# Rounding fp64 weights: the sign bits move from VectorE to GpSimd, the conversion is cut into four pieces, and the first attention pairs are planned closer

## The chip, the core and the metric

The kernel runs on one core of a Trainium2 chip. Its engines are TensorE (PE, with its weight loads as PEld), VectorE (DVE), ScalarE (ACT), GpSimd (POOL) and SyncE (SP), which here issues nearly all DMA transfers. The metric is the device time of one execution in microseconds (us); lower is better.

## What is computed

Two blocks follow each other. The first is attention with RMS-normalised queries and keys, over 8 batches, 12 heads, 448 positions and a head size of 64. The second is a SwiGLU feed-forward on the 3584 x 768 result, with 1536 hidden columns. The three weight matrices come in as fp64 numbers.

```python
q_n, k_n = rmsnorm(q, g_q), rmsnorm(k, g_k)
scores = (1 / sqrt(64)) * matmul(q_n, k_n.T)
attn = softmax(scores)
x = matmul(attn, v)                      # per head, then (B*S, H*D)
g = x @ w_gate
out = (silu(g) * (x @ w_val)) @ w_out
```

## The kernel before, in words

**Stages.** Two heads of a batch are a pair; there are 48. The first 12 pairs (`EARLY`, the first two batches) are computed alone, before any feed-forward. Then come four blocks of the feed-forward, each for two batches: an up part (gate and value products, line 1299) and a down part (line 1473). The attention of the next 12 pairs is woven into the down part of each block. The products use a scheme with 15 sub-products of 3 x 3 blocks: both the activations and the weights are first combined into 15 "sides". One up product is two matmuls of 128 x 448, with 120 products in a block (4 groups of 15 steps for gate and value).

**An early pair.** Queries and keys are loaded (line 728), squared on ACT (754), summed on DVE (768), turned into inverse roots (678 to 686), scaled on GpSimd (795), transposed on DVE (811) and, for queries, scaled again on ACT (814). PE makes the scores (840), ACT the exponentials (855), PE the weighted sums (916) and the sums of the weights (940). DVE takes reciprocals of these (975), PE spreads them over the rows (980), and DVE multiplies (1002). After six pairs DVE makes the activations' sides (1036 and 1040).

**Conversion of weights.** `convert` handles one of 24 parts of the fp64 weights (16 for the up part, 8 for the down part). A part is 128 x 1152 values, loaded as 64-bit words of which `lo` and `hi` are the two 32-bit halves. ACT makes a scaled copy of `hi` that drops the sign's and the exponent's upper part into place (line 1127) and scales `lo` (1131). Then DVE works on two halves of 576 values. For each it shifts the bits left by 3 (1147), takes the sign bit of `hi` and joins it to the bits (1150), and adds the rounded low part as an integer (1153). GpSimd makes the 15 sides of the weights in 12 instructions (1171 and 1174), and one store sends them to DRAM (1199), from where the blocks load them into `ws` (1260).

The first six conversions keep the shifted bits in SBUF. The other 18 (`by_bank`) put them into a PSUM bank (`st`), so that the instructions 1147, 1150 and 1153 have one operand in PSUM. The first conversions run beside the early pairs, all others beside block 0.

**Reads of the product banks.** Up products go to four PSUM banks, which DVE or ACT reads with one instruction for each product (ACT 1242 copies, DVE 1244 adds, 1246 subtracts, 1248 subtracts from the bank). Products of one chain go on accumulating in a bank, and the next may start only when the reading of the one before has ended. When a hidden value is complete ACT applies the silu (1373) and DVE multiplies (1376); line 1350 joins two partial results.

**What sets the order.** All of this is recorded as pieces, each with an engine, a planned duration, a due time and what it must come after. A planner (`Order.run`) walks through the pieces like a list scheduler and emits them one after the other. So it fixes the order of instructions on each engine at build time; each engine then runs its queue in that order, and an instruction that has to wait holds up all that stand behind it. A piece is emitted whole: nothing comes between its instructions on its engine. Due times (`when`) set priorities: the pairs are due `PAIR` us apart from `LEAD` on, and the due time of block 0 (`FIRST`) follows from these. `starts` and `spans` give the due times of the four groups of conversions; those of the second to fourth group are counted from `FIRST`. A piece marked `port` is kept apart from other pieces with that mark[...].

Of the kernel before, what the change touches and what calls it, by code (L numbers as in the profile page):

```python
# [360 lines left out]
class Order:  # L361
# [24 lines left out]
    def add(  # L386
        self, engine, us, when, emit, after=(), takes=(), uses=(), port=False, kb=0, group=None,
        mode=None, early=None, rank=0.0,
    ):
        piece = dict(  # L390
            engine=engine, us=us, when=when, emit=emit, takes=takes, port=port, kb=kb,
            group=group, mode=mode, early=early, rank=rank,
            after=[a for a in after if a is not None], end=None, n=len(self.pieces),
        )
        for tile_of in (*takes, *uses):
            self.users.setdefault(tile_of, []).append(piece)
        self.pieces.append(piece)
        return piece
# [79 lines left out]
def fast(  # L478
# [41 lines left out]
    nc = tc.nc  # L520
# [3 lines left out]
    P = 128  # L524
# [6 lines left out]
    TB = 512  # L531
# [23 lines left out]
    tiles = {}  # L555
# [10 lines left out]
    def take(name, key, shape):  # L566
        if name in ("e", "ea"):
            at = order.turn[name] % BUFS[name]
            tiles[name, key] = es[:, at] if at < BUFS["e"] else more_es[:, at - BUFS["e"]]
            return tiles[name, key]  # L570
        if name in OFTEN:
            at = OFTEN[name] + order.turn[name] % BUFS[name]
            tiles[name, key] = spare[:, ts(at, S)]
            return tiles[name, key]
        if name == "eh":
            at = order.turn["eh"] % BUFS["eh"]
            tiles[name, key] = more[:, at].rearrange("p (h q) -> p h q", h=2)
            return tiles[name, key]
        if name in WORK:
            at, size = WORK[name]  # L580
            at += order.turn[name] % BUFS[name] * size
            n = 1
            for length in shape[1:]:
                n *= length
            x = work[0 : shape[0], at : at + n]
            letters = "abcd"[: len(shape) - 1]
            x = x.rearrange(
                f"p ({' '.join(letters)}) -> p {' '.join(letters)}",
                **dict(zip(letters, shape[1:])),
            )  # L590
            tiles[name, key] = x
            return x
        pool = psum if name in ("st", "at") else sbuf
        tiles[name, key] = pool.tile(shape, F32, name=name, bufs=BUFS[name])
        return tiles[name, key]
# [37 lines left out]

    LEAD, PAIR = 14.0, 10.0
    FIRST = LEAD + EARLY * PAIR + 6.0
    PRODUCT = 1.504
    UP, DOWN, BOTH = 30 * NG * PRODUCT, 90.7, 170.0
# [449 lines left out]
    VALUES = 9 * P  # L1089
# [11 lines left out]
    def convert(key, src, sums, to, when, place, by_bank):  # L1101
# [3 lines left out]
        def add(*what, **more):  # L1105
            return order.add(*what, **dict(rank=rank, **more))
# [17 lines left out]
        bits = dst.bitcast(U32)  # L1124
        one = add(
            "ACT", 1.28, when,
            lambda: nc.scalar.activation(dst, hi.bitcast(F32), AF.Copy, scale=2.0**-111),
            after=[loaded],
        )
        two = add(  # L1130
            "ACT", 1.28, when, lambda: nc.scalar.activation(lo, lo, AF.Copy, scale=2.0**-29),
            after=[loaded],
        )


        bank = ("st", ("bits", key))

        def round_part(k, takes=False):
            if by_bank:
                if k == 0:  # L1140
                    take(*bank, [P, 2, TB])
                part = ts(k, VALUES // 2)
                to = tiles[bank].rearrange("p b t -> p (b t)")[:, 0 : VALUES // 2].bitcast(U32)
            else:
                part = ts(k, VALUES // 2)
                to = bits[:, part]
            nc.vector.tensor_scalar(
                out=to, in0=bits[:, part], scalar1=3, scalar2=None, op0=ALU.logical_shift_left
            )
            nc.vector.scalar_tensor_tensor(  # L1150
                to, hi[:, part], 0x80000000, to, op0=ALU.bitwise_and, op1=ALU.bitwise_or
            )
            nc.vector.tensor_tensor(out=bits[:, part], in0=to, in1=lo[:, part], op=ALU.add)

        last = one
        for k in range(2):
            last = add(
                "DVE", 2.28 if by_bank else 1.85, when, lambda k=k: round_part(k), after=[last, two],
                takes=[bank] if by_bank and k == 0 else [], uses=[bank] if by_bank and k else [],
                port=not by_bank,  # L1160
            )

        blocks = dst.rearrange("p (b f) -> p b f", f=P)
        b21, b31, b13, b23, b11, b12, b22, b32, b33 = (blocks[:, i] for i in range(9))
# [17 lines left out]
        for us, op in (  # L1182
# [21 lines left out]
    def up_weights(i, *how):  # L1204

        g, which, c = i // 4, i // 2 % 2, i % 2
        w = (moe_w_gate, moe_w_val)[which].rearrange("(c k p) (n f) -> p c k n f", p=P, k=3, n=3)
        weights["up", i] = convert(
            ("up", i), lambda k, n: w[:, c, k, n, ts(g, P)], UP_SUMS, up_sides[g][:, :, which, c],
            *how,  # L1210
        )

    def down_weights(i, *how):

        g, s = divmod(i, 2)
# [357 lines left out]
    for i in range(P // C):  # L1573
        h, half = divmod(i, 2)
# [4 lines left out]
            out=gg, in0=gq2, scalar=8.0 * GAIN**-2, in1=gk2, op0=ALU.mult, op1=ALU.mult  # L1579
# [5 lines left out]
    first = [(up_weights, i) for i in range(4 * NG)] + [(down_weights, i) for i in range(2 * NG)]  # L1585
    turns = [(*XS, *GT[:2], HS, SPARE), (ES, PAIRS, GT[2], SPARE, HS), (ES, PAIRS, HS, SPARE), (ES, HS)]
    starts = [LEAD - 4.0, FIRST - 20.0, FIRST + 60.0, FIRST + 110.0]
    spans = [16.0, 8.0, 9.0, 10.0]
    counts = [6, 10, 6, 2]
    todo = iter(first)  # L1590
    for n in range(4):
# [11 lines left out]
def kernel(  # L1603
# [63 lines left out]
```

## Time and profile before

The kernel takes 1500.53 us (median of three runs, 1499.26 to 1501.53). The profiled execution has a span of 1497.2 us.

| engine | busy us | share of the span | instructions |
|---|---|---|---|
| PE (matmul) | 1434.6 | 96% | 6672 |
| DVE | 916.9 | 61% | 1405 |
| ACT | 689.8 | 46% | 1372 |
| GpSimd | 408.8 | 27% | 468 |

| row | count | mean ns of one |
|---|---|---|
| GpSimd 1171, side of weights, 128x128, in es | 25 | 503 |
| GpSimd 1174, two sides, 128x256, in es | 10 | 822 |
| GpSimd 795, scaling of a pair, 128x448 | 96 | 1040 |
| GpSimd 860, sums, 128x896 | 36 | 2170 |
| DVE 975, reciprocals, 128x224, in the first 350 us | 12 | 1552 |
| PE 1299, up product, one matmul of 128x448 (mm) | 960 | 544 |

The first table shows which engine is full over the whole span; a mean over stages with different limits says little of one of them, so what a stage is worth is read from its own window. The second gives what single instructions last. A time in the columns "idle before" of the profile is charged to the wait that ended last, and idle time of an engine that isn't the bottleneck costs nothing by itself.

### The profile page before, as it was taken

To read this page: it belongs to the slowest core of one execution; us is meant where nothing else is said; L and a number is where in the kernel's file an instruction comes from. 1 tells how busy PE (TensorE), PEld (TensorE's weight loads), DVE (VectorE), ACT (ScalarE), POOL (GpSimd) and SP (SyncE) were. 2 spreads that over 40 slices of the span, in tenths; PEclk is the share of its full clock that TensorE was granted. 3 is DMA by queue.
4 is the path that set the end of the run, shared out by engine and by line. 5 is a ranking of instruction groups with operands and counts; after the bars stand their busy time and mean duration, and the time that the engine had idled before them with its cause. 6 is when DMAs were issued, how large, how long until landed. Compare 5 with 4: busy or idle time off the path is not lost.

```text
span 1497.2 us, 19504 instructions
## 1 busy us (share of the span) xinstructions
PE 1434.6 (96%) x6672; PEld 681.5 (46%) x6672; DVE 916.9 (61%) x1405; ACT 689.8 (46%) x1372; POOL 408.8 (27%) x468
## 2 busy tenths in 40 slices
PE   5898999799999999999999999999999999999998
PEld 2333444343344455554444445554444445555553
DVE  5867877868886743455876753453786854423533
ACT  6764544347777422254777432235677532122100
POOL 2562666544454300002344400002344410000000
PEclk9898999999999999999999999999999999999999
DMA  7675999974444342343453442343344343222235
GB/s 168 152 160 166 315 309 309 288 219 99 98 99 109 80 137 71 114 114 88 100 123 82 87 130 84 104 118 104 82 110 109 83 114 106 71 106 70 84 97 106
DMA packets 415922, 193.31 MB, mean 129 GB/s; under 512 B 324164, under 2 KB 397892, under 8 KB 409668
## 3 DMA queue, kind: packets, MB, share of 16 engines
q1 hardware_dynamic: 402688, 190.35, 47.5%
q10 hardware_dynamic: 12996, 1.61, 0.7%
q8 instruction: 55, 0.90, 0.3%
q14 instruction: 55, 0.45, 0.1%
q0 software_dynamic: 128, 0.00, 0.0%
HBM read 157.29 MB, written 34.60 MB: 128 GB/s over the span
## 4 chain that ended last, share of the span: by engine, by line
PE 73%; DVE 3%; ACT 1%; issue 1%; DMA 0%; SPq 0%; DVEq 0%; ACTq 0%
PE mm L1473 22%; PE mm L1299 19%; PE at L1299 19%; PE st L840 6%; PE at L916 6%; PE st L940 1%; DVE ss L684 0%; DMA out_dram<-spare 0%; ACT es L855 0%; DVE sums L866 0%; DVE ss L768 0%; DVE rd L975 0%; DVE ss L782 0%; DVE hs L1040 0%; ACT spare L990 0%
## 5 line engine op out<-in xcount | busy, mean ns | idle before, releaser
L1299 PE MATMUL mm<-xs,ws 128*128 128x448 f32 x960 | 405.0, 544 | 15.9 <-DVE gt L1248 9.9
L1299 PE MATMUL at<-xs,ws 128*128 128x448 f32 x960 | 400.7, 540 | 0.8 <-DVE v L1246 0.7
L1299 PEld LDWEIGHTS mm<-xs,ws 128*128 128x128 f32 x960 | 182.1, 191 | 199.4 <-issue 169.2
L1299 PEld LDWEIGHTS at<-xs,ws 128*128 128x128 f32 x960 | 182.3, 190 | 182.1 <-issue 174.5
L795 POOL TENSOR_TENSOR work<-work,rr 128x448 f32<-128x448 f32 x96 | 97.8, 1040 | 504.7 <-DVE rr L686 345.6
L1473 PE MATMUL mm<-gt,ws 128*128 128x448 f32 x448 | 175.7, 543 | 0.0
L840 PE MATMUL st<-work 64*64 64x448 f32 (+1 forms) x1536 | 154.8, 510 | 21.9 <-ACT work L814 15.6
L1244 DVE TENSOR_TENSOR gt<-gt,mm 128x448 f32<-128x448 f32 x64 | 39.7, 621 | 210.2 <-PE mm L1299 185.7
L1473 PE MATMUL mm<-hs,ws 128*128 128x448 f32 x384 | 151.0, 544 | 0.0
L855 ACT ACTIVATE es<-st 128x896 f32<-128x896 f32 x129 | 114.5, 915 | 75.5 <-PE at L916 52.2
L1373 ACT ACTIVATE st<-gt 128x448 f32<-128x448 f32 x96 | 52.6, 548 | 204.8 <-DVE gt L1248 104.4
L860 POOL TENSOR_TENSOR sums<-es 128x896 f32<-128x896 f32 x36 | 78.1, 2170 | 193.0 <-PE st L940 84.7
L990 ACT COPY spare<-rd 32x224 f32<-32x224 f32 x288 | 108.2, 376 | 47.3 <-DVE rd L975 42.1
L1473 PEld LDWEIGHTS mm<-gt,ws 128*128 128x128 f32 x448 | 83.5, 190 | 83.4 <-issue 80.5
L916 PE MATMUL at<-es,v 64*64 64x448 f32 x1032 | 115.0, 561 | 4.5 <-DVE xs L998 3.3
L1242 ACT COPY gt<-mm 128x448 f32<-128x448 f32 x80 | 42.6, 532 | 162.5 <-PE mm L1299 162.4
L1473 PEld LDWEIGHTS mm<-hs,ws 128*128 128x128 f32 x384 | 71.3, 190 | 71.4 <-issue 69.6
L840 PEld LDWEIGHTS st<-work 64*64 64x64 f32 x1536 | 52.0, 134 | 98.0 <-issue 35.7
L1242 ACT COPY v<-at 128x448 f32<-128x448 f32 x96 | 51.0, 531 | 76.1 <-PE at L1299 75.9
L860 POOL TENSOR_TENSOR sums<-sums,es 128x896 f32<-128x896 f32 x36 | 75.8, 2107 | 6.7 <-ACT es L855 4.1
L811 DVE STREAM_TRANSPOSE work<-work 128x448 f32<-128x448 f32 x96 | 58.7, 628 | 24.6 <-POOL work L795 15.1
L916 PEld LDWEIGHTS at<-es,v 64*64 64x64 f32 x1032 | 40.9, 138 | 67.7 <-issue 59.2
(141 smaller groups left out, 1581.6 us busy)
## 6 DMA issues: line engine op xcount, KB each, us to landing
ws<-up_sides SPq DMA_DIRECT2D x32, 1024.0 KB, 4.9
ws<-down_sides SPq DMA_DIRECT2D x16, 1024.0 KB, 4.9
ws<-down_sides SPq DMA_DIRECT2D x28, 512.0 KB, 4.0
ws<-up_sides SPq DMA_DIRECT2D x16, 768.0 KB, 4.4
work<-in_q_dram SPq DMA_DIRECT2D x192, 56.0 KB, 2.3
work<-in_k_dram SPq DMA_DIRECT2D x188, 56.0 KB, 2.3
out_dram<-spare SPq DMA_DIRECT2D x168, 56.0 KB, 1.9
v<-in_v_dram SPq DMA_DIRECT2D x96, 96.0 KB, 2.4
```

Source lines behind the costliest of these rows:

```text
L795: nc.gpsimd.tensor_tensor(out=tiles["t", m][:, x], in0=tiles["qk", (m, x)], in1=rr.to_broadcast([P, NC, C]), op=ALU.mult,)
L811: nc.vector.transpose(to, tiles["t", m][:, x].rearrange("p c f -> p (c f)"))
L840: nc.tensor.matmul(st[ds(D * x, D), h, 0:n], tiles["KT", m][rows, ds(P * j + D * of_keys, D)], tiles["QT", m][rows, ds(Q * of_queries, n)] ...
L855: nc.scalar.activation(e, tiles["st", (m, j)][:, :, 0 : S * width(j) // P], AF.Exp)
L860: nc.gpsimd.tensor_tensor(out=to, in0=tiles["e", (m, 0)] if j == 1 else to, in1=e, op=ALU.add)
L916: nc.tensor.matmul(tiles["at", (m, x)][ds(D * h, D), queries], tiles["v", m][rows, j, h], tiles["e", (m, j)][rows, h], start=j == 0, stop= ...
L990: nc.scalar.copy(inv[ds(D * h + C * to, C), ts(x, Q)], tiles["rd", m][ds(D * h + C * x, C)])
L1242: nc.scalar.copy(to, ps)
L1244: nc.vector.tensor_tensor(out=to, in0=old, in1=ps, op=ALU.add)
L1299: nc.tensor.matmul(ps(), w[:, at, which, c], xs[:, SLOT[x], c], start=fresh and c == 0, stop=c == NC2 - 1, skip_group_check=True,)
L1373: nc.scalar.activation(take(*act, [P, 2, TB])[:, 0, 0:S], to, AF.Silu)
L1473: nc.tensor.matmul(banks[s][:, 0:S], w[:, at, s, g], where[x][:, g], start=fresh and g == 0, stop=g == NG - 1, skip_group_check=True,)
```

## The change

For each conversion GpSimd now turns `hi` in place into an integer that holds the sign bit alone: it compares with 0 and multiplies by 2^31, with an unsigned integer as output. That is one instruction over all 1152 values. DVE then needs two instructions for each half instead of three: the shift and the joining of the sign become one (`shift`), and the integer addition stays (`round_part`). Each of these is a piece of its own, so that a conversion is four pieces of DVE work where it was two, and the planner may put other work between them. The first pairs are due 9 us apart instead of 10, and the first six conversions 13 us apart instead of 16.

```diff
--- before.py
+++ after.py
@@ -633,7 +633,7 @@
 
 
 
-    LEAD, PAIR = 14.0, 10.0
+    LEAD, PAIR = 14.0, 9.0
     FIRST = LEAD + EARLY * PAIR + 6.0
     PRODUCT = 1.504
     UP, DOWN, BOTH = 30 * NG * PRODUCT, 90.7, 170.0
@@ -1131,34 +1131,46 @@
             "ACT", 1.28, when, lambda: nc.scalar.activation(lo, lo, AF.Copy, scale=2.0**-29),
             after=[loaded],
         )
+        three = add(
+            "POOL", 1.6, when,
+            lambda: nc.gpsimd.tensor_scalar(
+                out=hi, in0=hi.bitcast(F32), scalar1=0.0, scalar2=2.0**31, op0=ALU.is_lt,
+                op1=ALU.mult,
+            ),
+            after=[one], port=True,
+        )
 
 
         bank = ("st", ("bits", key))
 
-        def round_part(k, takes=False):
-            if by_bank:
-                if k == 0:
-                    take(*bank, [P, 2, TB])
-                part = ts(k, VALUES // 2)
-                to = tiles[bank].rearrange("p b t -> p (b t)")[:, 0 : VALUES // 2].bitcast(U32)
-            else:
-                part = ts(k, VALUES // 2)
-                to = bits[:, part]
-            nc.vector.tensor_scalar(
-                out=to, in0=bits[:, part], scalar1=3, scalar2=None, op0=ALU.logical_shift_left
-            )
+        def half(k):
+            part = ts(k, VALUES // 2)
+            if not by_bank:
+                return part, bits[:, part]
+            bank_of = tiles[bank].rearrange("p b t -> p (b t)")
+            return part, bank_of[:, 0 : VALUES // 2].bitcast(U32)
+
+        def shift(k):
+            if by_bank and k == 0:
+                take(*bank, [P, 2, TB])
+            part, to = half(k)
             nc.vector.scalar_tensor_tensor(
-                to, hi[:, part], 0x80000000, to, op0=ALU.bitwise_and, op1=ALU.bitwise_or
-            )
+                to, bits[:, part], 3, hi[:, part],
+                op0=ALU.logical_shift_left, op1=ALU.bitwise_or,
+            )
+
+        def round_part(k):
+            part, to = half(k)
             nc.vector.tensor_tensor(out=bits[:, part], in0=to, in1=lo[:, part], op=ALU.add)
 
         last = one
         for k in range(2):
-            last = add(
-                "DVE", 2.28 if by_bank else 1.85, when, lambda k=k: round_part(k), after=[last, two],
-                takes=[bank] if by_bank and k == 0 else [], uses=[bank] if by_bank and k else [],
-                port=not by_bank,
-            )
+            for x, op in enumerate((shift, round_part)):
+                last = add(
+                    "DVE", 0.77 if by_bank else 0.9, when, lambda k=k, op=op: op(k),
+                    after=[last, two, three], takes=[bank] if by_bank and not k and not x else [],
+                    uses=[bank] if by_bank and (k or x) else [], port=not by_bank,
+                )
 
         blocks = dst.rearrange("p (b f) -> p b f", f=P)
         b21, b31, b13, b23, b11, b12, b22, b32, b33 = (blocks[:, i] for i in range(9))
@@ -1585,7 +1597,7 @@
     first = [(up_weights, i) for i in range(4 * NG)] + [(down_weights, i) for i in range(2 * NG)]
     turns = [(*XS, *GT[:2], HS, SPARE), (ES, PAIRS, GT[2], SPARE, HS), (ES, PAIRS, HS, SPARE), (ES, HS)]
     starts = [LEAD - 4.0, FIRST - 20.0, FIRST + 60.0, FIRST + 110.0]
-    spans = [16.0, 8.0, 9.0, 10.0]
+    spans = [13.0, 8.0, 9.0, 10.0]
     counts = [6, 10, 6, 2]
     todo = iter(first)
     for n in range(4):
```

More of the change, by code (lines that the diff above doesn't have):

```diff
@@ L1133, in convert @@
         )
-        bank = ("st", ("bits", key))
-        def round_part(k, takes=False):
-            if by_bank:
-                if k == 0:
-                    take(*bank, [P, 2, TB])
-                part = ts(k, VALUES // 2)
-                to = tiles[bank].rearrange("p b t -> p (b t)")[:, 0 : VALUES // 2].bitcast(U32)
-            else:
-                part = ts(k, VALUES // 2)
-                to = bits[:, part]
-            nc.vector.tensor_scalar(
-                out=to, in0=bits[:, part], scalar1=3, scalar2=None, op0=ALU.logical_shift_left
-            )
-            nc.vector.scalar_tensor_tensor(
-                to, hi[:, part], 0x80000000, to, op0=ALU.bitwise_and, op1=ALU.bitwise_or
-            )
+        three = add(
[6 more added lines that the diff above has]
+        )
+        bank = ("st", ("bits", key))
+        def half(k):
[8 more added lines that the diff above has]
+            part, to = half(k)
+            nc.vector.scalar_tensor_tensor(
+                to, bits[:, part], 3, hi[:, part],
+                op0=ALU.logical_shift_left, op1=ALU.bitwise_or,
+            )
+        def round_part(k):
+            part, to = half(k)
             nc.vector.tensor_tensor(out=bits[:, part], in0=to, in1=lo[:, part], op=ALU.add)
```

## The prediction

> **What bounds the kernel now.** I first read the page's slices, 37.4 us each: they tell in which stage TensorE isn't full.
>
> ```profile
> PE   5898999799999999999999999999999999999998
> DVE  5867877868886743455876753453786854423533
> POOL 2562666544454300002344400002344410000000
> PEclk9898999999999999999999999999999999999999
> DMA  7675999974444342343453442343344343222235
> ```
>
> From the tenth slice on PE stands at 9; only the first nine (to about 340 us) hold anything to win, and there VectorE is at 5 to 8, GpSimd at 2 to 6 and DMA at 5 to 9. To split them by stage I cut at the first product of block 0 (149.3) and its last (353.7), read from the PE timeline. The columns are busy us of PE, PEld, DVE, ACT and POOL, then PE clock, DMA share, GB/s.
>
> ```profile
> 0.00:149.30 149.30, 115.21 (x1201) 49.27 (x1202) 99.57 (x175) 92.23 (x181) 64.89 (x105) 0.92 0.68 161
> 149.30:353.70 204.40, 188.64 (x505) 92.21 (x504) 159.48 (x244) 97.49 (x137) 118.60 (x224) 0.97 0.89 272
> 353.70:1484.00 1130.30, 1125.00 (x4955) 537.38 (x4954) 654.30 (x982) 500.09 (x1054) 225.27 (x140) 1.00 0.39 100
> ```
>
> The third stage is 99.5% PE: its 1130 us stay, and what the first two win or lose ends in the total one for one. The early pairs have 149.3 - 115.2 = 34.1 us of PE idle, 14.7 of it before the first matmul, so 19.4 inside. Block 0 has 204.4 - 188.6 = 15.8 us. Then the waits of PE in the first 400 us (total us, times, longest):
>
> ```profile
> PE mm L1299 <- DVE gt L1248: 9.9, 2, 6.7
> PE mm L980 <- DVE ss L684: 5.7, 3, 2.7
> PE mm L980 <- DVE rd L975: 4.2, 2, 2.5
> PE mm L1299 <- DVE gt L1244: 4.1, 2, 2.2
> ```
>
> All four name VectorE. L980 is the spreading of a pair's reciprocals; where L684 is named, it ran just after the reciprocal L975 that the spread needs. The longest wait of block 0 shows the mechanism, PE first, then DVE over the same time:
>
> ```profile
> 289.56 1.77 PE L1299 MATMUL at<-xs,ws 128*128 128x448 f32 x4 [0.66 <-DVE v L1246]
> 298.05 3.36 PE L1299 MATMUL mm<-xs,ws 128*128 128x448 f32 x4 [6.72 <-DVE gt L1248]
> ```
> ```profile
> 292.60 0.75 DVE L1147 TENSOR_SCALAR st<-work 128x576 uint32<-128x576 uint32 x1
> ...
> 296.71 0.75 DVE L1153 CUSTOM_DVE_ANT_0 work<-work,st 128x1152 uint16<-128x1152 uint16 x1
> 297.38 0.62 DVE L1248 TENSOR_TENSOR gt<-mm,gt 128x448 f32<-128x448 f32 x1
> ```
>
> PE stands until L1248 has read the bank; L1248 stands behind both halves of a conversion (six instructions, 4.8 us) in DVE's queue. The 3.2 us gap before 195.9 looks alike. The pair 298.05 (3.36 for four matmuls) against 1.67 elsewhere shows a second cost: a half-speed spell after a gap. In the early stage it is larger: busy x (1 - clock) over 49.3-73.3, 73.3-116.7 and 116.7-149.3 gives 20.3 x 0.14 + 37.3 x 0.07 + 28.5 x 0.16 = 10 us; in block 0, over the two stretches with the gaps, 3.2 x 0.27 + 20.4 x 0.11 = 3 us.
>
> **What the Trainium skill says.** "TensorE: Matmul & The Clock Gate", Part 1: TensorE falls to half clock after an idle window of some 3.4 us and comes back after as long a busy one. The trace agrees on the factor (539 ns against up to 1116 for one product matmul) but gaps of 2.5 and 2.7 us were enough here. "SBUF — State Buffer", Who interferes with whom: a VectorE instruction with two SBUF inputs contends with a GpSimd instruction that reads SBUF, one with a single SBUF input does not. The trace agrees: L1150 with one SBUF input takes 762 ns with little spread, with two it means 894 and 930 and reaches 1.17 us. "GPSIMD Engine Reference", Elementwise — side-by-side cycle accounting: 1.03 cycles per element where only the port limits, about 1.8 for a tight loop, 2.6 with two inputs, at 1.2 GHz. No GpSimd tensor_scalar is in the trace; two-input adds there agree roughly (2170 ns for 896 elements).
>
> ```profile
> L1147 DVE TENSOR_SCALAR st<-es 128x576 uint32<-128x576 uint32 x10 | 7.6, 756 | 0.1
> L1150 DVE SCALAR_TENSOR_TENSOR st<-es,st 128x576 uint32<-128x576 uint32 x10 | 7.6, 762 | 0.6
> L1150 DVE SCALAR_TENSOR_TENSOR xs<-xs 128x576 uint32<-128x576 uint32 x4 | 3.6, 894 | 0.1
> ```
>
> **The change part by part.**
>
> The removed VectorE shift (L1147): 36 in the 18 conversions through a bank, 7.6 + 6.0 + 6.0 + 4.5 + 3.0 = 27.1 us by their rows, and 12 in the first six, 2.1 + 2.6 + 1.1 + 0.8 = 6.6 us. The first 27 lie in block 0 in front of bank reads, thus on PE's path at the gaps; the 6.6 lie in the early stage, partly in front of reciprocals.
>
> The shift that stays now reads bits and signs, two SBUF inputs, also in the conversions through a bank. Bounds: 0.76 (undisturbed) to 1.17 (slowest seen), 0 to 0.41 x 36 = 14.8 us given back. I take 0.15 each, 5.4 us, as in the early rows (894 - 762). VectorE's work in block 0 becomes 159.5 - 27.1 + 5.4 = 138 us.
>
> The sign on GpSimd: 1152 elements, one input. Skill's cycles: 0.99 (1.03) to 2.5 us (2.6); I take 1.8 cycles, 1.7 us (an estimate), since a compare and a product are more than a copy. 24 x 1.7 = 41 us, 31 of them in block 0: GpSimd there 118.6 + 31 + 5 = 155 us of some 193, 80%. It is a new wait between ACT's copy and VectorE's shift. Queued behind a sign on GpSimd are the pairs' scalings (L795) early, and the side sums of the conversion before in block 0; behind a shift that waits for it on VectorE stand the bank reads for which PE waits. The built order puts most signs ahead of the previous conversion's twelve sums (2.08 + 0.87 + 0.46 + 1.29 + 0.46 + 0.73 + 0.46 = 6.35 us), so I count no wait for them in the forecast; the rival below does.
>
> Four pieces in place of two: a bank read now can slip in after 0.8 us of conversion where it had 2.3 before. The built order uses that for some conversions (one read between pieces), while others still stand as four pieces in a row, 3.0 us against 4.6. So a gap like the 6.7 us one shrinks by 1.5 to 4 us. Of block 0's 15.8 + 3 = 19 us I take 10: the five gaps lose 1.5 to 3 us each (some 10 us with the half-speed spells), the rest stays.
>
> Pairs planned at 9 and the first six conversions at 13: every due time up to block 0 moves, block 0's by 12. Due times don't make work shorter; what they change is the order. In the built order the spread L980 of most pairs moves behind the scores or weighted sums of the next pair, so the reciprocal has 3 us or more. Spread waits are 5.7 + 4.2 + 0.4 = 10.3 us; the last (1.68) stays, as nothing stands between, 8.6 goes, and with it some 7 of the 10 us at low clock: 15.6. Against it the compressed stage has new waits: six signs of 1.7 us before scalings, DMA share 0.68 that rises by a tenth, conversions 3 us closer. I take 5.6 for these and keep 10. The floor leaves room: 14.7 + 115.2 - 10 = 120 us against 149.3.
>
> DMA: share 0.99 in block 0's first 43 us, and its load of the second group's weights (issued at 187.6, 5 to 6 us to landing) arrives 44.5 us into the block, where 30 products of 1.504 need 45.1. A block without the first gap has this transfer just in time. The last down weights land at about 341 for a need at 353.7. For both I take off 1 us.
>
> Sum: 10 + 10 - 1 = 19; 1500.5 - 19 = 1481.5, forecast **1482**.
>
> **Rivals.** *Early waits only move* (the scalings wait for signs and loads, PE's gaps reappear before scores): block 0's 10 minus 0 to 1 alone, 1490. For it: PE already waits behind ACT and DMA in many small gaps there. Against it: the spreads, more than half of the idle, are taken off the path.
>
> *GpSimd becomes the bound*, slower: at 2.5 us a sign plus 0.8 for two blocked accesses, one conversion costs GpSimd 6.35 + 2.5 + 0.8 = 9.65 us, where the conversions now follow each other every (317.1 - 157.1) / 17 = 9.4. The chain ends 17 x 0.25 = 4 us later, VectorE stands at the shifts with bank reads behind it (one added us at each of five gaps), and early six signs of 2.5 take 15 against the 15.6 won: 1500.5 + 4 + 5 - 1 = 1508. For it: GpSimd would be at (118.6 + 45 + 15) / 193 = 93%. Against it: it has 86 idle us in block 0 now.
>
> *All is recovered*: 15.6 early, 16 of 19 in block 0: 1469. DMA at 0.99 speaks against it.
>
> **How the numbers follow.** Forecast 0.46, early waits only move 0.22, all recovered 0.12, GpSimd the bound 0.20. The first three are faster, 0.80; of the last I put a quarter within 0.2% (a sign between 1.7 and 2.5), 0.05, and 0.15 slower. The range 1468 to 1502 reaches just past the full recovery and up to no change, leaving the slower cases out.
>
> **What would show it.** First product of block 0 at about 139 us, its last at 332 (block 193 us); spread waits near 2 us; no PE wait of more than 4 us on L1248's counterpart; shift 0.85 to 0.95 us; sign 1.5 to 1.9 us; PE clock above 0.95 before block 0; the third stage within 3 us of 1130. Wrong if signs take over 2.2 us, if VectorE's shifts stand waiting for GpSimd with reads behind them, or if PE's waits turn to weight transfers at group starts.

## The result, and the profile after

The changed kernel takes 1552.88 us (median, 1551.59 to 1553.73), the kernel before 1499.89 us on the same chip: a ratio of 1.036, 95% interval 1.033 to 1.039. The forecast was 1482 us; the time lies above its range and above every rival.

The page's slices of the changed kernel, 38.8 us each:

```profile
PE   4778977887799999999999999999999999999998
DVE  5667685565699574345577674345687674333543
POOL 3685698888354420001244420001243420000000
PEclk9989988988899999999999999999999999999999
DMA  7755868775544443244244452244345352222235
```

PE reaches its 9 for good only in the twelfth slice, and has mostly 7 and 8 where it had 9. Block 0 lies in the slices 5 to 10: there GpSimd rises to 8 and 9 (it had 4 to 6), while VectorE is down to 5 and 6 in the last four and DMA, which had 9, to 5 to 8. The same by stage, cut at the first up product, the first down product and the end; columns as in the prediction (busy us of PE, PEld, DVE, ACT, POOL, then PE clock, DMA share, GB/s):

```profile
0.00:157.10 157.10, 114.03 (x1201) 50.64 (x1202) 103.67 (x163) 92.53 (x181) 93.60 (x114) 0.92 0.66 155
157.10:401.60 244.50, 201.07 (x482) 97.26 (x480) 154.14 (x196) 82.82 (x113) 197.38 (x234) 0.90 0.73 226
401.60:1550.50 1148.90, 1135.07 (x4992) 542.80 (x4992) 660.21 (x1000) 509.57 (x1074) 226.52 (x144) 0.99 0.39 99
```

The early stage is 7.8 us longer, block 0 is 40.1 us longer (244.5 against 204.4), the rest 5.4 us: 53.3 in all. Of the 5.4, 4.3 us are PE work that the new order moved out of block 0 (1135.1 us busy against 1130.7). GpSimd has 79 us more to do in block 0 and DMA falls from 0.89 to 0.73 of the time, so the DMA engines aren't the new bound. PE stands 244.5 - 201.1 = 43.4 us in block 0 where it stood 15.8. The rest of the loss is hidden in its busy time: 482 records of matmuls (four are one product) take 201.1 us at a clock of 0.90, while e1 below, which keeps the order, has 483 in 183.5 us at 0.99. So some 17 us are matmuls that ran slowly, like those after the gap shown below. The waits of PE in the first 410 us (total us, times, longest):

```profile
PE mm L1311 <- DVE gt L1256: 19.4, 3, 8.2
PE at L1311 <- DVE v L1256: 9.9, 3, 5.4
PE mm L1311 <- DVE gt L1260: 9.2, 3, 4.2
PE at L916 <- DVE xs L998: 9.0, 3, 4.8
...
PE mm L980 <- DVE rd L975: 3.2, 3, 2.2
...
PE mm L1485 <- DMA ws<-down_sides: 2.8, 1, 2.8
```

Lines have moved by 12: L1311 is the up product, L1256 and L1260 are reads of its banks. The waits for the spreads L980 did go, from 10.3 to 3.2 us; the large ones for bank reads grew from 14.0 to 38.5. In the early stage waits came up elsewhere: the weighted sums L916 wait 9.0 us for L998, which joins the two halves of a pair's sums (3.3 before), and the waits for exponentials (L855) went from 7.0 to 11.9 us. One wait for a bank read, PE first, then GpSimd and VectorE over the same time (start, duration, instruction, in brackets the idle time before it and who ended it):

```profile
299.64 1.67 PE L1311 MATMUL at<-xs,ws 128*128 128x448 f32 x4
306.05 3.35 PE L1311 MATMUL mm<-xs,ws 128*128 128x448 f32 x4 [4.74 <-DVE gt L1256]
```
```profile
297.66 0.45 POOL L1186 TENSOR_TENSOR es<-es 128x128 f32<-128x128 f32 x1
298.08 4.21 POOL L1136 TENSOR_SCALAR work<-work 128x1152 uint32<-128x1152 f32 x1
```
```profile
292.33 0.62 DVE L1256 TENSOR_TENSOR v<-v,at 128x448 f32<-128x448 f32 x1 [0.88 <-PE at L1311]
302.32 0.77 DVE L1157 SCALAR_TENSOR_TENSOR st<-work 128x576 uint32<-128x576 uint32 x1 [9.37 <-POOL work L1136]
...
305.38 0.61 DVE L1256 TENSOR_TENSOR gt<-gt,mm 128x448 f32<-128x448 f32 x1
```

Read from the end: PE needs the read L1256, which stands in VectorE's queue behind four pieces of a conversion; the first of them, the shift L1157, waits 9.37 us for the sign; GpSimd starts this only when the sums of the conversion before are done, and needs 4.21 us for it. The pieces don't help, since nothing had been placed between them here. VectorE's waits for signs come to 53.5 us. The groups (busy us, mean ns of one, idle before):

```profile
L1136 POOL TENSOR_SCALAR es<-es 128x1152 uint32<-128x1152 f32 x5 | 21.4, 4276 | 10.3 <-DMA gt<-in_moe_w_gate_dram 10.3
```
```profile
L1157 DVE SCALAR_TENSOR_TENSOR st<-gt 128x576 uint32<-128x576 uint32 x4 | 12.2, 3058 | 10.9 <-POOL gt L1136 10.9
L1157 DVE SCALAR_TENSOR_TENSOR st<-es 128x576 uint32<-128x576 uint32 x10 | 12.1, 1215 | 7.8 <-POOL es L1136 7.6
L1157 DVE SCALAR_TENSOR_TENSOR st<-work 128x576 uint32<-128x576 uint32 x8 | 7.6, 946 | 12.8 <-POOL work L1136 12.7
```

A sign takes 4.2 to 4.4 us. The shift is 0.76 us by itself but 3.06 on the mean in one place; single ones show why, here VectorE's and then GpSimd's:

```profile
251.96 4.40 DVE L1157 SCALAR_TENSOR_TENSOR st<-gt 128x576 uint32<-128x576 uint32 x1 [5.12 <-POOL gt L1136]
```
```profile
251.89 4.20 POOL L1136 TENSOR_SCALAR spare<-spare 128x1152 uint32<-128x1152 f32 x1
```

The shift's own sign is ready, but GpSimd started the next one 0.07 us earlier, and the shift, with two SBUF inputs, ends only after it. Below, such a lengthened instruction is said to be held up. In the early stage the small instruction L782 (two SBUF inputs) goes from a mean of 171 to 965 ns in the same way:

```profile
L782 DVE SCALAR_TENSOR_TENSOR ss<-ss 128x28 f32<-128x28 f32 x12 | 11.6, 965 | 3.4 <-ACT ss L778 3.1
```

### The profile page after: what moved, and what is told of

Its sections match the earlier page's. It is cut to its first block, busy times and chain, and to the rows that moved or that the text cites. A ratio compares the mean times of both kernels' runs of the same rounds, so it can differ in the third digit from the quotient of the medians.

```text
span 1550.5 us, 19481 instructions
## 1 busy us (share of the span) xinstructions
PE 1450.2 (94%) x6672; PEld 690.7 (45%) x6672; DVE 918.0 (59%) x1357; ACT 684.9 (44%) x1368; POOL 517.5 (33%) x492
## 4 chain that ended last, share of the span: by engine, by line
PE 70%; DVE 1%; ACT 1%; SPq 1%; DMA 1%; issue 0%; ACTq 0%; DVEq 0%
PE mm L1485 22%; PE at L1311 17%; PE mm L1311 17%; PE st L840 6%; PE at L916 6%; PE st L940 1%; DMA out_dram<-spare 0%; SPq L728 0%; ACT es L855 0%; DVE rd L975 0%; DVE ss L782 0%; DVE spare L1533 0%; DMA work<-in_q_dram 0%; DVE xs L1040 0%; DVE work L811 0%
## 5 line engine op out<-in xcount | busy, mean ns | idle before, releaser
L1311 PE MATMUL mm<-xs,ws 128*128 128x448 f32 x960 | 411.4, 552 | 30.5 <-DVE gt L1256 19.4
L1311 PE MATMUL at<-xs,ws 128*128 128x448 f32 x960 | 408.9, 549 | 11.1 <-DVE v L1256 9.9
L1311 PEld LDWEIGHTS mm<-xs,ws 128*128 128x128 f32 x960 | 184.7, 194 | 218.1 <-issue 172.6
L1311 PEld LDWEIGHTS at<-xs,ws 128*128 128x128 f32 x960 | 185.9, 194 | 196.6 <-issue 180.4
L1385 ACT ACTIVATE st<-gt 128x448 f32<-128x448 f32 x96 | 52.5, 547 | 234.5 <-DVE gt L1260 121.4
L1256 DVE TENSOR_TENSOR gt<-gt,mm 128x448 f32<-128x448 f32 x64 | 39.7, 621 | 186.6 <-PE mm L1311 186.6
L855 ACT ACTIVATE es<-st 128x896 f32<-128x896 f32 x129 | 114.7, 915 | 70.4 <-PE at L916 50.4
L916 PE MATMUL at<-es,v 64*64 64x448 f32 x1032 | 117.6, 555 | 9.4 <-DVE xs L998 6.5
L1254 ACT COPY gt<-mm 128x448 f32<-128x448 f32 x80 | 42.5, 531 | 165.4 <-PE mm L1311 165.4
L1254 ACT COPY v<-at 128x448 f32<-128x448 f32 x96 | 51.0, 531 | 76.6 <-PE at L1311 76.4
L916 PEld LDWEIGHTS at<-es,v 64*64 64x64 f32 x1032 | 41.9, 137 | 72.1 <-issue 59.8
```

Source lines behind the costliest of these rows:

```text
L855: nc.scalar.activation(e, tiles["st", (m, j)][:, :, 0 : S * width(j) // P], AF.Exp)
L916: nc.tensor.matmul(tiles["at", (m, x)][ds(D * h, D), queries], tiles["v", m][rows, j, h], tiles["e", (m, j)][rows, h], start=j == 0, stop= ...
L1254: nc.scalar.copy(to, ps)
L1256: nc.vector.tensor_tensor(out=to, in0=old, in1=ps, op=ALU.add)
L1311: nc.tensor.matmul(ps(), w[:, at, which, c], xs[:, SLOT[x], c], start=fresh and c == 0, stop=c == NC2 - 1, skip_group_check=True,)
L1385: nc.scalar.activation(take(*act, [P, 2, TB])[:, 0, 0:S], to, AF.Silu)
```

## The experiments

The theory after the traces (A): the sign's length on GpSimd is the cause. It can act in three ways: VectorE waits for the sign, VectorE is held up by it, and GpSimd's load delays all that follows the sides of the weights. The rival (B) is the plan: closer due times and another order. The table has the profiled run's stages (first up product; to the first down product; the rest) and the ratio of the timed runs to the kernel before, which was timed again beside each group of runs (1496.5 to 1499.9 us). A stage is read from one execution: two of the same kernel (e4 and e14) differ by 2.3, 0.3 and 1.5 us.

| kernel | early | block 0 | rest | median us | ratio (95%) |
|---|---|---|---|---|---|
| before | 149.3 | 204.4 | 1143.5 | 1499.9 | 1 |
| after | 157.1 | 244.5 | 1148.9 | 1552.9 | 1.036 (1.033-1.039) |
| e1 short sign | 152.1 | 194.4 | 1147.9 | 1497.5 | 1.0011 (0.9993-1.0029) |
| e2 old due times | 162.3 | 244.3 | 1147.6 | 1555.0 | 1.0377 (1.0348-1.0406) |
| e3 closer alone | 145.8 | 209.9 | 1144.0 | 1501.7 | 1.0036 (1.0025-1.0047) |
| e4 pieces alone | 140.3 | 200.8 | 1145.5 | 1488.3 | 0.9938 (0.9918-0.9959) |
| e4b pieces, closer | 151.2 | 199.9 | 1145.0 | 1497.7 | 1.0001 (0.9986-1.0017) |
| e5 right price | 151.3 | 261.1 | 1137.4 | 1553.8 | 1.0382 (1.0355-1.0410) |
| e6 fills | 151.8 | 231.2 | 1148.8 | 1536.3 | 1.0255 (1.0230-1.0280) |
| e6b sign unused | 160.8 | 227.4 | 1149.1 | 1537.8 | 1.0253 (1.0232-1.0274) |
| e11 fills unused | 149.4 | 221.6 | 1147.9 | 1526.1 | 1.0200 (1.0168-1.0231) |
| e9 fast sign | 156.1 | 197.1 | 1147.9 | 1501.3 | 1.0020 (1.0011-1.0030) |
| e10 fast sign, old due times | 159.1 | 202.1 | 1146.0 | 1507.0 | 1.0049 (1.0034-1.0063) |
| e8b sign on ScalarE, old due times | 161.9 | 195.3 | 1148.0 | 1505.7 | 1.0052 (1.0031-1.0073) |
| e12 fast sign in block 0 | 141.7 | 200.5 | 1144.3 | 1490.5 | 0.9955 (0.9938-0.9971) |
| e13 the same, conversions earlier | 143.1 | 204.9 | 1140.5 | 1490.8 | 0.9963 (0.9951-0.9974) |
| e14 pieces alone again | 142.6 | 201.1 | 1147.0 | 1491.5 | 0.9965 (0.9951-0.9979) |

**e1: the sign an eighth as long.** Order of every engine as in the changed kernel.

```diff
-                out=hi, in0=hi.bitcast(F32), scalar1=0.0, ...
+                out=hi[:, 0:144], in0=hi[:, 0:144].bitcast(F32), scalar1=0.0, ...
...
-                to, bits[:, part], 3, hi[:, part],
+                (the shift reads the first 144 signs four times)
```

> The changed kernel with the order of every engine kept, but the sign made of the first 144 values alone, which then serve for all 1152 (so the signs of the other values are left out). GpSimd's sign shrinks from 4.2 us to an estimated 0.55 (4.2 x 144/1152 and a little fixed cost). Theory A, the length of the sign is the cause: GpSimd in block 0 falls from 197 to some 132 us, VectorE's waits for the sign from 53 us to under 8, the shift through a bank from 0.9-3.1 us on the mean to 0.8-0.9, the early stage from 157 to 141-147 us, block 0 from 242 to 193-200 us, and the time to 1482-1492, below the kernel before. Theory B, the plan (closer due times, four pieces in another order) is the cause: the time stays above 1525. A result of 1500-1520 would divide the cause.

The sign took 0.72 us, and 52 of the 53 us are gone: the length is the cause. But the time is that of before, not below it. Block 0 did gain 10 us (half of it PE work that now lies in the rest); the early stage lost 2.8 instead of gaining 10.

**e2: the changed kernel with the old due times; e3: the closer due times alone.**

```diff
-    LEAD, PAIR = 14.0, 9.0        (e2; e3 is the reverse, in the kernel before)
+    LEAD, PAIR = 14.0, 10.0
-    spans = [13.0, 8.0, 9.0, 10.0]
+    spans = [16.0, 8.0, 9.0, 10.0]
```

> The changed kernel with the due times of before (pairs 10 us apart, first six conversions 16). Theory A, the sign's length: still slow, 1540-1555, with the sign at 4.2 us; the early stage at 150-157 us, block 0 still above 235. Theory B, the closer due times bring the loss: within 5 us of the kernel before, 1495-1505.

> The kernel before with nothing but the closer due times (9 and 13). Theory A: the spreads of the reciprocals come off PE's path as in the changed kernel (10.3 us of waits before, 3.2 there), the first product of block 0 comes at 139-144 us in place of 149, and the time is 1488-1495. Theory B: closer due times collide with transfers and conversions, 1505-1530.

e2 is as slow as the change, so the due times aren't the cause. e3 is 0.36% slower than before: theory A's side expectation failed too. The spread waits fell from 10.3 to 5.1 us, but others came: these two lines of e3 had 15.6 and 1.0 us before, and 3.4 us of waiting for weights (L1299 on `up_sides`) are new.

```profile
PE st L840 <- ACT work L814: 19.5, 8, 14.6
...
PE at L916 <- ACT es L855: 6.2, 3, 4.2
```

**e4: the pieces alone; e4b: pieces and closer due times.** The kernel before with its three VectorE instructions for a half as three pieces.

```diff
-            last = add("DVE", 2.28 if by_bank else 1.85, when, lambda k=k: round_part(k), ...)
+            for x, op in enumerate((shift, sign, round_part)):
+                last = add("DVE", 0.77 if by_bank else 0.63, when, lambda k=k, op=op: op(k), ...)
```

> The kernel before with the three VectorE instructions of each half as three pieces (six for a conversion in place of two), nothing else. Theory A: bank reads slip in between the pieces, block 0's gaps shrink from 15.8 us to 6-12 and the time is 1490-1498. Rival: the reads are held up by the banks and the transfers anyway, and the time stays within 3 us of 1500. Theory B: a plan with more pieces is worse, above 1505.

> The kernel before with the conversion in pieces and the closer due times. The pieces alone brought 8 us, the due times alone cost 5. If the two are independent, 1490-1496; if the pieces take away what the due times collide with, the early stage falls below 138 us and the time to 1478-1486; if the due times cost more with more pieces, above 1500.

The pieces are worth 0.6% (0.35% when run again, e14 below), but not where I had looked: 9 us in the early stage, 3.6 in block 0, whose two largest gaps stand as before (6.4 and 3.2 us). With the closer due times on top the gain is gone: the early stage goes back from 140.3 to 151.2 us.

**e5: the planner told the sign's true length.** `"POOL", 1.6` becomes `"POOL", 4.3`.

> The changed kernel with the planner told that a sign takes 4.3 us in place of 1.6, which is its measured length. Theory A1, a plan on a wrong price: the planner kept shifts too close behind the signs, and with the right price it places other VectorE work there; VectorE's waits for signs fall from 53 us to under 25 and the time to 1505-1525. Theory A2, capacity and blocking: GpSimd needs 4.2 + 6.4 us for each conversion and VectorE is held up by the signs whatever the order; the time stays within 12 us of 1555, 1540-1560, waits for signs above 35 us.

VectorE's waits for signs fell from 53.5 to 21.0 us, as A1 says, yet the time stayed, as A2 says. The 36 shifts through a bank, 27.4 us at 0.762 each, took 47.7 us in the changed kernel and 58.5 here: 20 us of hold-ups became 31. So the right price in the plan took waits away and brought hold-ups, and the conversions as a whole ended no sooner: their last store comes 246.3 us after the first up product, against 234.1 in the changed kernel.

**e7: what a GpSimd instruction over 1152 elements costs.** Forms one to a line, after GpSimd's last own work.

> The kernel before, with GpSimd instructions over 1152 elements added after its last own work, one form to a line, each three times: the sign as it is (every second word, unsigned output), over 576 elements, on neighbouring words, with a float output, then product and addition in float, one product in float on neighbouring and on every second word, and fills. From 4.23 us for 1152 and 0.72 for 144 elements the sign costs 3.5 ns an element and 0.2 fixed; so 576 should take 2.2 us. If the compare or the integer output is what is slow, product and addition take 2 us or less; if two operations are, only the single products do (1.0-1.7); if the stride is, the neighbouring words take half of 4.2; if every tensor_scalar on GpSimd goes at this pace, all forms take 3.5-4.3.

```profile
L1609 POOL TENSOR_SCALAR work<-work 128x1152 uint32<-128x1152 f32 x3 | 12.3, 4105 | 0.0
L1615 POOL TENSOR_SCALAR work<-work 128x1152 f32<-128x1152 f32 x3 | 10.2, 3394 | 0.0
L1614 POOL TENSOR_SCALAR work<-work 128x1152 f32<-128x1152 f32 x3 | 9.7, 3219 | 0.2
L1608 POOL TENSOR_SCALAR work<-work 128x576 uint32<-128x576 f32 x3 | 6.7, 2220 | 0.2
L1613 POOL TENSOR_SCALAR work<-work 128x1152 f32<-128x1152 f32 x3 | 3.6, 1194 | 0.0
L1612 POOL MEMSET work<- 128x1152 f32 x3 | 3.4, 1143 | 0.0
```

L1609 is the sign on neighbouring words (4.1 us; 4.2 with a float output, and 4.4 on every second word as in the kernel: means, as in the row; so neither stride nor output type matters much), L1608 the sign of 576 elements, L1614 and L1615 a product alone (3.2 and, on every second word, 3.4), L1613 product and addition: 1.19. So it matters which operations are asked for, and the single product costs more than product and addition in one. Why, no run shows. This led to a cheap sign.

**e9 and e10: the fast sign.** A product with 0 and the addition of -0 leave a float whose only bit is the sign; e10 has the old due times.

```diff
-                out=hi, in0=hi.bitcast(F32), scalar1=0.0, scalar2=2.0**31, op0=ALU.is_lt,
-                op1=ALU.mult,
+                out=hi.bitcast(F32), in0=hi.bitcast(F32), scalar1=0.0, scalar2=-0.0, op0=ALU.mult,
+                op1=ALU.add,
```

> The changed kernel, order of every engine kept, with the sign made by another pair of operations on GpSimd: product with 0, then addition of -0, float output, which leaves the sign bit alone. The separate measurement had product and addition at 1.15 us on neighbouring words and some 0.13 more for every second word, so a sign of 1.3 us in place of 4.2. Theory A, the length is the cause: between the shortened sign (0.72 us, 1497.5) and a little above it, 1496-1504, block 0 at 194-200 us, VectorE's waits for signs under 8 us. Theory B, the operation's kind or its place in the plan: above 1530.

> The same fast sign with the due times of before (10 and 16 us). If the closer due times cost what they cost the kernel with pieces alone (9 us), 1485-1492, and the early stage at 140-146 us; if the sign in GpSimd's queue costs the early stage by itself, whatever the due times, 1495-1506.

e9 keeps the order of every engine and all of the computation: a sign of 1.23 to 1.27 us (medians of its groups) in place of 4.2 takes 3.4 percentage points off. e10, just above its second range, is worse than e9, though the old due times were better in e4 against e4b: there the first up product comes at 159.1, after 11.8 us of waiting for its weights.

**e8b: the sign on ScalarE.**

```diff
-            lambda: nc.gpsimd.tensor_scalar(out=hi, ...)
+            "ACT", 1.28, when, lambda: nc.scalar.activation(hi.bitcast(F32), hi.bitcast(F32), AF.Copy, scale=0.0),
```

> The changed kernel with the sign made by ScalarE (a copy scaled by 0, whose float result has the sign bit alone) in place of GpSimd, and the due times of before. ScalarE's copies of the same size take 1.1-1.3 us in the trace; 24 of them add some 30 us to an engine at 97 of 204 us in block 0. Theory A (the sign's length on GpSimd is the cause, the removed VectorE shift is worth its 27 us of block 0 in part): no VectorE wait for a sign above 2 us, early stage 140-145, block 0 190-198, time 1475-1487, below the pieces alone (1488). Rival: ScalarE's queue (exponentials, copies of banks) gets the new wait, time 1490-1505.

ScalarE's copy dropped the sign bit: the outputs deviate exactly as those of e6 do, where all signs are 0. So it is read for time alone. Each sign took 1.26 us, VectorE waited 14.7 us for them, and block 0 fell to 195.3, but the first up product waited 14.8 us for its weights and the early stage took 161.9.

**e6, e6b and e11: waiting, hold-ups and load taken apart.** Order of every engine kept.

```diff
-            lambda: nc.gpsimd.tensor_scalar(out=hi, ...)                       (e6, e11)
+            lambda: [nc.gpsimd.memset(hi.bitcast(F32)[:, 0:n], 0.0) for n in (VALUES, VALUES, VALUES, 700)],
-                to, bits[:, part], 3, hi[:, part],                             (e6b, e11)
+                to, bits[:, part], 3, lo[:, part],
```

> The changed kernel, order kept, with each sign replaced by four fills of hi with zeros on GpSimd (1152, 1152, 1152 and 700 words; by the separate measurement 1.14 us for 1152, so 4.1 us in all); all signs are left out. The fills take as long as the sign and VectorE waits for them as for the sign, but they read nothing. Theory A1, the time is GpSimd's length in the chain: 1540-1558 still, waits for the fills 40-60 us. Theory A2, the sign holds VectorE's instructions with two SBUF inputs up for its whole length: no VectorE instruction of 4.4 us any more, the shift at 0.75-1.0 us on the mean, and the time falls to 1515-1535.

> The changed kernel, order kept, with the sign made as it is (4.2 us) but not used: VectorE's shift joins lo in place of it, so VectorE no longer waits for GpSimd's sign (the values' signs are wrong). GpSimd's work and the hold-ups remain. Theory A1, VectorE's wait in order behind the sign is the cause: the 53 us of waits go and the time falls to 1500-1515. Theory A3, GpSimd has too much work (10.7 us for each of 18 conversions, and the sides of the weights come late): PE waits for transfers of weights in place of VectorE, and the time stays above 1530.

> The changed kernel, order kept, with the four fills in place of the sign (4.1 us, nothing read) and VectorE's shift joining lo, so that it neither is held up by the sign nor waits for it (all signs are left out). Only GpSimd's load remains: 4.1 + 6.4 us for each conversion. If wait and hold-up stand in for each other and the load alone is harmless, 1498-1508. If GpSimd's load alone makes the sides of the weights late, 1520-1536, with GpSimd busy above 190 of some 225 us of block 0.

With fills no shift through a bank took over 1.28 us any more (4.46 in the changed kernel), and the group that had 3058 ns has

```profile
L1157 DVE SCALAR_TENSOR_TENSOR st<-gt 128x576 uint32<-128x576 uint32 x4 | 3.1, 764 | 7.6 <-POOL gt L1137 7.6
```

while VectorE still waited 55 us for them, and the time, 1536.3 us, lies between the two expectations. So the hold-ups need GpSimd to read. "SBUF — State Buffer" in the Trainium skill says so (Who interferes with whom: a GpSimd instruction that only writes doesn't contend with VectorE's two-input ones), and this agrees. Without the wait (e6b) the time stayed above 1530, as A3 says, and the hold-ups grew: the shifts in `hs` went from a mean of 1314 to 2092 ns.

From the ratios, in us of 1498: load alone, e11 against e1, 1.0200 - 1.0011 = 28; the wait on top, e6, 8; the hold-ups on top, e6b, 8; both, the changed kernel, 24. Each of these differences is uncertain by 5 to 7 us to either side, so the single terms of 8 are barely clear of noise, and the waits and hold-ups together cost more than the two terms say. That load alone is about half stands well clear. How load alone costs time when nobody waits for the sign can be followed through one gap of e11, in SyncE's queue, then ScalarE, VectorE and PE:

```profile
257.95 2.80 SPq L1272 DMA_DIRECT2D ws<-up_sides  x2
273.30 0.53 SPq L1211 DMA_DIRECT2D up_sides<-hs  x1
273.87 3.58 SPq L1117 DMA_DIRECT2D spare<-in_moe_w_out_dram  x3
```
```profile
283.40 1.24 ACT L1127 ACTIVATE spare<-spare 128x1152 f32<-128x1152 f32 x1 [9.81 <-DMA spare<-in_moe_w_out_dram]
...
285.66 0.52 ACT L1385 ACTIVATE st<-gt 128x448 f32<-128x448 f32 x1
286.13 0.52 ACT L1254 COPY w<-mm 128x448 f32<-128x448 f32 x1
```
```profile
286.22 0.62 DVE L1388 SCALAR_TENSOR_TENSOR gt<-st,v 128x448 f32<-128x448 f32 x1 [9.46 <-ACT st L1385]
```
```profile
286.70 2.72 PE L1311 MATMUL mm<-xs,ws 128*128 128x448 f32 x4 [4.66 <-ACT w L1254]
```

The store of the sides in `hs` stands in SyncE's queue until GpSimd has made them (12.4 us by the waits). The load of the next raw part into `spare` is queued behind it, so ScalarE waits 9.81 us for it; the silu L1385 and the bank copy L1254 stand behind that, VectorE waits for the silu, PE for the copy. Four queues in order pass a late GpSimd on to PE.

**e12, e13 and e14: where the gain of a short sign goes.** e12 is e4 with the fast sign in the 18 conversions beside block 0 alone. e13 pulls their due times together. e14 is e4 again.

```diff
+        three = None
+        if by_bank:
+            three = add("POOL", 1.3, when, lambda: ... (fast sign), after=[one], port=True)
-    starts = [LEAD - 4.0, FIRST - 20.0, FIRST + 60.0, FIRST + 110.0]        (e13)
-    spans = [16.0, 8.0, 9.0, 10.0]
+    starts = [LEAD - 4.0, FIRST - 20.0, FIRST + 50.0, FIRST + 92.0]
+    spans = [16.0, 7.0, 7.0, 7.0]
```

> The kernel in pieces with the due times of before, the sign on GpSimd by product and addition (1.26 us) in the 18 conversions beside block 0 alone; the first six keep their three VectorE instructions for a half. The early stage has the order of the kernel in pieces (140.3 us there). If the early stage is where the sign's place in GpSimd's queue costs, the early stage stays at 139-142, block 0 goes from 200.8 to 194-198 and the time is 1478-1486, below the pieces alone (1488.3). If the sign costs block 0 what it saves VectorE, 1487-1493.

> The kernel with fast signs beside block 0 alone, with the due times of the conversions in block 0 pulled together (7 us apart in place of 8, 9 and 10, the groups 10 and 18 us earlier). If the chain of conversions (load, ScalarE, VectorE, GpSimd, store, load of weights) only came too late by its due times, the 7.5 us wait before the down part shrinks below 3 us and the time falls to 1480-1487. If the chain runs as fast as transfers and engines let it, the wait stays above 5 us or moves into the block, and the time is 1487-1496.

> The kernel in pieces once more, beside the other: 1485-1491.

e12's early stage stayed at 141.7, so it is the early conversions with signs (and two VectorE pieces for a half in place of three) that made it long in e10 (159.1). Block 0 didn't gain (200.5; 200.8 and 201.1 in e4 and e14), although PE's waits for bank reads fell to two of 2.2 and 2.3 us. The last transfers of the conversions and PE in e12, then the same stores and loads in e13:

```profile
331.93 0.52 SPq L1224 DMA_DIRECT2D down_sides<-es  x1
337.02 1.29 SPq L1285 DMA_DIRECT2D ws<-down_sides  x3
```
```profile
342.24 5.49 PE L1498 MATMUL mm<-hs,ws 128*128 128x448 f32 x8 [7.49 <-issue]
```
```profile
331.96 0.52 SPq L1224 DMA_DIRECT2D down_sides<-hs  x1
337.06 0.82 SPq L1285 DMA_DIRECT2D ws<-down_sides  x2
```

In e12 PE has finished block 0's up products and stands 7.49 us, until the last sides are stored (5.1 us from the store to the load behind it) and loaded back (5.2 more). The wait bears the name "issue"; in e1, e9 and e10 the wait at this place names the load of `down_sides`, 4.3 to 6.1 us. So the row of conversions has become the limit: no down product without the sides of the last one.

The row's length, from the first up product to its last store, in us: 173 to 182 where GpSimd makes no sign in block 0 (e4b 173.4, e4 176.9, e14 177.8, before 181.3, e3 182.2); 184 to 192 with a short sign (e1 184.2, e9 186.5, e13 188.9, e12 190.2, e10 191.7); 211 to 234 where each keeps GpSimd for 4.2 us (e11 211.3, e6b 216.9, e6 221.0, the changed kernel 234.1, e2 234.3). In the first group PE is later than the transfers. In the other two, e13 apart, 10 to 11 us more for store and load are the length of block 0. So in the changed kernel too the row sets the end of the block, here its last store and PE:

```profile
391.19 0.52 SPq L1211 DMA_DIRECT2D down_sides<-es  x1
```
```profile
401.55 6.29 PE L1485 MATMUL mm<-hs,ws 128*128 128x448 f32 x8 [2.82 <-DMA ws<-down_sides]
```

The last store comes 234.1 - 181.3 = 52.8 us later than before. Before, the weights had 12.7 us of room; the difference is the 40.1 us that block 0 lost. Inside the block PE meets the same row earlier, as waits for reads that stand behind shifts.

Earlier due times (e13) left the last store at the same microsecond, as a row does that runs as fast as its steps let it; the sign is one step more in it. Which step sets its pace wasn't taken apart. In e13 the weights weren't the last thing that PE waited for. The planner had put the scores of the next pair in front of the down products, and these waited for their scaled queries, so that block 0 came to 204.9 us:

```profile
343.45 4.59 PE L840 MATMUL st<-work 64*64 64x224 f32 x32 [9.01 <-ACT work L814]
```

So the pieces with the old due times, without fast signs (e4, e14) or with them beside block 0 (e12, e13), are 0.35 to 0.6% faster than the kernel before, and these versions can't be told apart.

## Why the prediction was wrong

**The sign's price is the step that failed.** "I take 1.8 cycles, 1.7 us", with 2.5 as the upper bound, was 4.2 to 4.4 us. "GPSIMD Engine Reference" in the Trainium skill (Elementwise — side-by-side cycle accounting) gives 1.03 to 2.6 cycles an element. At the 1.2 GHz of that page 4.25 us are 4.4 cycles; product and addition on neighbouring words fit in the page's span (1.19 us, 1.2 cycles), a compare with a product (4.3) and a product alone (3.4) don't. The figures there are for an addition of two tensors and for loops of a few operations; I carried them over to an instruction that neither page nor trace showed, and then took their ends for bounds. With a sign of 1.25 us, below the price that I took, e9 stands at 1.0020 of the kernel before in place of 1.036. So this step made some 51 of the 71 us between 1482 and 1553; the other 20 are the forecast gain, which didn't come with a cheap sign either; the paragraphs from the due times on say why.

**"I count no wait for them"** rested on that price: 53.5 us of waits. I had argued from the order, in which most signs stand ahead of the sums before them; the one of the example stands behind the sums of two conversions (284.6 to 298.1 us on GpSimd), and a sign in front of sums delays those instead.

**"0.15 each, 5.4"** for the second SBUF input was 20 us in the shifts through a bank, plus 9.5 in L782. A hold-up lasts as long as the other engine's instruction, so its bound was the sign's length and not the slowest shift seen beside short ones.

**Due times: "keep 10".** The spread waits fell as forecast, but with the due times alone (e3) the early stage gained 3.5 us and block 0 lost 5.5, and with pieces they cost 0.35 to 0.6%. The rival in which early waits only move has this right.

**Pieces: "take 10" in block 0.** Alone they gave 3.6 and 3.3 us there (e4, e14), and 9.0 and 6.7 in the early stage, where I had expected nothing of them.

**The removed shift: 27.1 us on PE's path at the gaps.** With a short sign the gaps did close (e1, e12), but then the row of conversions set the end of block 0. I had seen the last weights land at 341 us for a need at 353.7, 12.7 us of room, and took off 1 us for them and the second group's. Not only did the need come earlier; the sign, a step more in the row, made the weights later as well.

**The rival "GpSimd becomes the bound"** had the mechanism. Its sum with 4.2 us in place of 2.5: 6.35 + 4.2 + 0.8 = 11.35 us for a conversion, 17 x (11.35 - 9.4) = 33; early signs 25 against 15.6 won, 10; reads 5; less 1: 1547, close to 1553. So near a sum is in part luck: the row's last store came 52.8 us later, not 33, and the rival took off nothing for the 12.7 us of room. That its three ways of acting are load (about half), wait and hold-up was found by the runs.

What stays open: why the early stage comes out at 140 to 162 us with small changes of the plan. Signs in the first six conversions lengthen it (e10 159.1 against e12 141.7), and with signs and the old due times (e2, e8b, e10) the first weights come late: PE waits 11.8 to 14.8 us for them. Closer due times lengthen it with pieces alone (140.3 to 151.2) and shorten it elsewhere (e3 by 3.5, the changed kernel by 5.2 against e2). Which decision of the planner does it wasn't tried. Open is also why a compare and a single product are slow on GpSimd.

## What to carry to other kernels

Price an operation that no trace shows by a run of its own in the very form it will have (operations, types, size); otherwise let the range reach past the page's figures. When work moves to an engine in the middle of a chain, follow its queue onward: loads behind stores, copies behind loads, bank reads behind copies. And before counting a closed gap as gain, look how much room the next limit leaves, here the last weights, 12.7 us, and whether the change takes from this room too.

## What the runs showed of the hardware

On GpSimd, over 128x1152 floats, product and addition took 1.19 us, a product alone 3.22, and a compare with a product 4.1 to 4.4; the sign over 144 elements took 0.72, so 3.5 ns an element with 0.2 us beside. A fill took 1.14 us and held none of VectorE's two-input shifts up (764 ns on the mean in `gt`), while a GpSimd instruction of 4.20 us that reads made one of 0.76 us last 4.40. On GpSimd product with 0 and addition of -0 left the sign bit (e9); on ScalarE a copy scaled by 0 left none (e8b). The half-speed spell after a gap isn't set by the gap alone: the four records of an up product took 1.77 us after PE had stood 3.07 us in e6b, 2.84 after 2.42 us in e6, and 3.35 after 4.74 in the changed kernel.
